# Windowed attention into an ELU feed-forward layer: v and k loaded as float32 by ScalarE's queue and cast by GpSimd, q and k transposed by DMA, a new static order

## The chip, the cores and the metric

The kernel runs on 1 core of a Trainium2 chip. The metric is the device time of one execution in microseconds (us). A core has five engines with instruction queues of their own: PE (TensorE, matmuls and transposes), DVE (VectorE), ACT (ScalarE), POOL (GpSimd) and SP (SyncE, which only issues DMAs here). ACT and POOL issue DMAs too, and an engine that issues one does so in its place among its other instructions.

## The reference

```python
# q, k, v: [8 batches, 8 heads, 576 tokens, 64] float32
scores = q @ k.transpose(0, 1, 3, 2) / 8
scores = where(abs(pos[:, None] - pos[None, :]) <= 32, scores, -1e9)
attn = softmax(scores)                       # per row
x = (attn @ v).transpose(0, 2, 1, 3).reshape(4608, 512)
h = x @ w_in                                 # [512, 2048]
g = where(h > 0, h, exp(minimum(h, 0)) - 1)  # ELU
out = g @ w_out                              # [2048, 512], float32
```

All arrays come and go as float32; the kernel computes in bfloat16 with float32 accumulation.

## The kernel before

**Units of work.** A batch is nine blocks of 64 queries (`QB`). A block of queries sees the 128 keys from 32 before it to 32 behind it. Two blocks are a *pair* of 128 tokens: 36 pairs, four and a half to a batch. Pairs are gathered into ten *tiles* of the feed-forward layer: tiles 0 and 1 have two pairs each (256 tokens), tiles 2 to 9 four (512 tokens).

**Attention.** For each batch, q and k come as float32 by four DMAs (`load_qk`, L155; half the heads each; 96 partitions, 6 tokens to a partition), issued by SP for batch 0 and by ACT later. `cast` (L168, L170) makes bfloat16 of them, on POOL from batch 1 on. `T` (L180) transposes them on PE, six matmuls against the identity for one pair of heads, eight such groups to a batch; `E` (L193 on ACT, L195 on DVE) copies each group out of PSUM into `kT` and `qT`. v comes by POOL's queue, cast to bfloat16 on the way (`load_v`, L203), the even blocks only; the odd blocks are the same rows moved by half the partitions, copied inside SBUF by DVE in batches 0 and 1 (`copy_v`) and by two DMAs of SP later (`shift_v`, L210, L212). For each pair: `QK` (L239) computes the transposed scores into `psS`, `SM` (L247, ACT) their exponential, `MK` (L260, DVE) multiplies by the mask into `pm`, `AV` (L272, PE, two groups of heads) multiplies by v, where a column of ones gives the row sums, `RN` (L285, L287, DVE) divides by them. `X` turns the pair's result round into `xt`, tokens in the free dimension: by PE for the first four pairs (L302, L308), by a DMA transpose of SP for the others (L298).

**Feed-forward.** For each tile and each of 16 slices of 128 hidden features: `H` (L319) is four matmuls into one of three `psH` buffers, `EX` (L327, ACT) the exponential, `FF` (L339, DVE; L337, ACT, for the odd slices of tiles 0 and 1) cuts it at zero, `GG` (L348 or L345, DVE) takes the larger of it and h and so frees the `psH` buffer. `Y` (L362) accumulates 16 matmuls for one pair of the tile before, in four parts of four; `YC` (L368, ACT) copies the result and `OUT` (L373, SP) stores it. Both weight matrices are loaded in four pieces each by POOL's queue, with a cast (`WI` L394, `WO` L399).

**What sets the order.** Nothing is scheduled while the kernel runs. The class `Plan` takes every operation with an engine, a duration, a rank and what it depends on, plays them through once while the program is built, and emits them in the order of this play; each engine then runs its list in that order and waits with semaphores. Where an engine stands at an instruction whose operand is not there, all that is behind it on that engine waits too. `H`'s in PE's list are mixed with `Y`'s of the tile before and with the attention of pairs about a tile ahead.

Of the kernel before, what the change touches and what calls it, by code (L numbers as in the profile page):

```python
# [20 lines left out]
class Plan:  # L21
# [4 lines left out]
    LAT = 0.25  # L26

    def __init__(self):
        self.ops = {}

    def op(self, name, eng, dur, rank, deps, fn, dma=0.0, lag=0.0,
           at=0.0):


        self.ops[name] = (eng, dur, rank, tuple(deps), fn, dma, lag, at)

    def run(self):
        ops = self.ops
        done, users, left = {}, {}, {}
        for n, o in ops.items():  # L40
            left[n] = len(o[3])
            for d in o[3]:
                assert d in ops, (n, d)
                users.setdefault(d, []).append(n)
        free = {}
        server = 2.0
        ready = {}
        for n, o in ops.items():
            free.setdefault(o[0], 0.0)
            if left[n] == 0:  # L50
                ready.setdefault(o[0], {})[n] = 0.0
        order = []
        while len(order) < len(ops):
            best = None
            for e, rs in ready.items():
                if not rs:
                    continue
                t = max(free[e], min(rs.values()))
                n = min((ops[n][2], n) for n, r in rs.items() if r <= t)[1]
                if best is None or t < best[0]:  # L60
                    best = (t, e, n)
            t, e, n = best
            del ready[e][n]
            _, dur, _, _, fn, dma, lag, at = ops[n]
            free[e] = t + dur
            if dma:
                server = max(server, t + dur) + dma
                end = server + 2.0 + lag
            else:
                end = t + dur + lag  # L70
            end = max(end, at)
            done[n] = end
            order.append((t, n))
            for u in users.get(n, ()):
                left[u] -= 1
                if left[u] == 0:
                    ue = ops[u][0]
                    r = max(done[d] + (0.0 if ops[d][0] == ue
                                       and not (ops[d][5] or ops[d][6] or ops[d][7]) else self.LAT)
                            for d in ops[u][3])  # L80
                    ready.setdefault(ue, {})[u] = r
        self.done = done
        self.order = order
        for _, n in order:
            ops[n][4]()
# [3 lines left out]
def kernel(  # L89
# [20 lines left out]
    PR = 96  # L110
    TPP = S // PR
    KW = S + 2 * WIN
# [4 lines left out]
    VW = D + 1  # L117

    const = ctx.enter_context(tc.tile_pool(name="const", bufs=1))
    stg = ctx.enter_context(tc.tile_pool(name="stg", bufs=4))  # L120
    bfp = ctx.enter_context(tc.tile_pool(name="bfp", bufs=4))
# [12 lines left out]

    ident = const.tile([128, 128], BF16)
    masks = const.tile([128, 4, QB], BF16)
# [3 lines left out]
    NVB = 3  # L140
    NPB = 2
    kT = [const.tile([128, HP, KW], BF16, name=f"kT{i}") for i in range(NKB)]
    qT = [const.tile([128, HP, S], BF16, name=f"qT{i}") for i in range(NKB)]
    vw = [const.tile([128, NQB, H, VW], BF16, name=f"vw{i}") for i in range(NVB)]
    pm = [const.tile([128, H, 3 * QB], BF16, name=f"pm{i}") for i in range(NPB)]

    live = {}
    EVAC = {(nm, hp): "DVE" if (nm, hp) == ("k", 3) else "ACT"
            for nm in "qk" for hp in range(HP)}


    def load_qk(b, nm, half, eng):
        src = {"q": q, "k": k}[nm]
        t = stg.tile([PR, HP, TPP * D], FP32, name="stg", tag="stg")
        eng.dma_start(  # L155
            out=t, in_=src[b, half * HP:(half + 1) * HP].rearrange(
                "h (p t) d -> p h (t d)", t=TPP))
        live[nm, b, half] = t

    def cast(b, nm, half, eng):  # L160
        if (nm, b) not in live:
            live[nm, b] = bfp.tile([PR, TPP, H, D], BF16, name="bf", tag="bf")
        t = live[nm, b]
        src = live.pop((nm, b, half)).rearrange("p h (t d) -> p h t d", t=TPP)
        dst = t[:, :, half * HP:(half + 1) * HP, :].rearrange(
            "p t h d -> p h t d")
        if eng is nc.scalar:
            nc.scalar.copy(dst, src)  # L168
        else:
            eng.tensor_copy(dst, src)  # L170

    def T(b, nm, hp):
        src = live[nm, b]
        n = 2 * hp + (nm == "k")
        if b == 0 and n % 4:
            pt = psH_p.tile([128, TPP, PR], BF16, name="psH", tag="psH")
        else:
            pt = psT_p.tile([128, TPP, PR], BF16, name="psT", tag="psT")
        for j in range(TPP):
            nc.tensor.transpose(pt[:, j, :], src[:, j, 2 * hp:2 * hp + 2, :],  # L180
                                ident[0:PR, 0:PR])
        live["T", b, nm, hp] = pt

    def E(b, nm, hp):
        pt = live.pop(("T", b, nm, hp))
        if nm == "k":
            dst = kT[b % NKB][:, hp, WIN:WIN + S]
        else:
            dst = qT[b % NKB][:, hp, :]
        dst = dst.rearrange("c (p t) -> c p t", t=TPP)  # L190
        src = pt.rearrange("c t p -> c p t")
        if EVAC[nm, hp] == "ACT":
            nc.scalar.copy(dst, src)  # L193
        else:
            nc.vector.tensor_copy(dst, src)  # L195


    def load_v(b, qb):
        vt = vw[b % NVB]
        vb = v[b].rearrange("h s d -> s h d")  # L200
        lo, hi = max(0, qb * QB - WIN), min(S, qb * QB - WIN + 128)
        r = lo - (qb * QB - WIN)
        nc.gpsimd.dma_start(out=vt[r:r + hi - lo, qb, :, 0:D], in_=vb[lo:hi])  # L203

    def swapped(b, qb):
        return b < 2 and qb % 2 == 1

    def shift_v(b, w0, w1):
        vt = vw[b % NVB]
        nc.sync.dma_start(out=vt[0:QB, w0:w1 - 1:2],  # L210
                          in_=vt[QB:128, w0 - 1:w1 - 1:2])
        nc.sync.dma_start(out=vt[QB:128, w0:w1 - 1:2],  # L212
                          in_=vt[0:QB, w0 + 1:w1:2])

    def copy_v(b, w0, w1, part, eng):


        vt = vw[b % NVB]
        if part == 0:
            eng.tensor_copy(vt[0:QB, w0:w1 - 1:2], vt[0:QB, w0 + 1:w1:2])  # L220
        else:
            eng.tensor_copy(vt[QB:128, w0:w1 - 1:2],
                            vt[QB:128, w0 - 1:w1 - 1:2])


    def QK(i):
        psS = psS_p.tile([128, 2, 2, HP, QB], FP32, name="psS", tag="psS")
        for s in range(2):
            b, qb = divmod(2 * i + s, NQB)
            for h in range(H):  # L230
                hp, base = h // 2, 64 * (h % 2)
                rhs = qT[b % NKB][base:base + 64, hp, qb * QB:qb * QB + QB]
                lo = qb * QB
                if swapped(b, qb):
                    parts = ((0, QB, lo + QB), (QB, 128, lo))
                else:
                    parts = ((0, 128, lo),)
                for p0, p1, c in parts:
                    nc.tensor.matmul(  # L239
                        psS[p0:p1, h % 2, s, hp, :],  # L240
                        lhsT=kT[b % NKB][base:base + 64, hp, c:c + p1 - p0],
                        rhs=rhs, start=True, stop=True)
        live["S", i] = psS

    def SM(i):
        pu = pup.tile([128, 2, 2, HP, QB], BF16, name="pu", tag="pu")
        nc.scalar.activation(pu, live.pop(("S", i)), AX.Exp, scale=SCALE)  # L247
        live["U", i] = pu

    def MK(i):  # L250
        pu = live.pop(("U", i))
        p = pm[i % NPB]
        for s in range(2):
            b, qb = divmod(2 * i + s, NQB)
            m = masks[:, 1 if qb == 0 else 2 if qb == NQB - 1 else
                      3 if swapped(b, qb) else 0, :]
# [73 lines left out]
    def fact(t, fo):  # L330
        return t < 2 and fo % 2 == 1
# [43 lines left out]

# [9 lines left out]
    NC0 = 4  # L385

    P = Plan()
# [13 lines left out]


    PER = 8.0
    LEAD = 20.0

    def prank(i):
        return PER * tiles[where[i][0]][0] + PER * (i - tiles[where[i][0]][0]) - LEAD - 16

    casts0 = {("q", 0): "DVE", ("k", 0): "ACT", ("q", 1): "DVE",
              ("k", 1): "POOL"}  # L410
    engs = {"DVE": nc.vector, "ACT": nc.scalar, "POOL": nc.gpsimd}
    cdur = {"DVE": 1.2, "ACT": 1.5, "POOL": 1.5}
    LAND = {(0, "k", 0): 6.2, (0, "q", 0): 8.7, (0, "k", 1): 11.0,
            (0, "q", 1): 14.0, (1, "k", 0): 33.0, (1, "q", 0): 36.0,
            (1, "k", 1): 39.0, (1, "q", 1): 42.0}
    SVOF = {}
    L1AT = 2
    for b in range(B):
        need = prank(b * NQB // 2)
        r0 = need - 60  # L420
        t0 = where[b * NQB // 2][0]
        early = [("H", max(t0 - 2, 0), 2 if b == 2 else 8)] if b > 1 else []
        for half in range(2):
            for nm in ("q", "k"):
                deps = list(early)
                if b == 1:
                    deps.append(("SM", L1AT))
                if b:
                    deps.append(("C", b - 1, nm, half))
                P.op(("L", b, nm, half), "ACT" if b else "SP", 0.1,  # L430
                     r0 + half, deps,
                     lambda b=b, nm=nm, half=half: load_qk(
                         b, nm, half, nc.scalar if b else nc.sync),
                     dma=0.0 if b < 2 else 2.2,
# [228 lines left out]
```

The softmax here doesn't subtract the row's maximum and nothing guards it: scores larger than these inputs give would overflow.

## Time and profile before

| | |
|---|---|
| time, two runs | 366.52 and 367.85 us, median 367.19 |
| profiled execution | span 364.3 us from the first to the last instruction; the page gives no other time of it, so 2.9 us lie between its span and the median of the runs |
| PE busy | 315.6 us (87%) |
| DVE busy | 253.8 us (70%) |
| ACT busy | 185.0 us (51%) |
| POOL busy | 87.8 us (24%) |
| TensorE clock granted, mean | 0.986 |
| DMA queues, share of 16 engines' span | POOL's (q0) 32.6%, SP's (q1) 22.3%, ACT's (q10) 18.4% |
| PE matmuls of `T` (L180, into psT and psH) | 25.5 and 3.6 us busy |
| ACT's copies of `E` (L193), DVE's (L195) | 35.6 and 6.1 us busy |
| POOL casts of q and k (L170) | 42.9 us busy, 29 of them |
| POOL DMA issues for v (L203) | 35.5 us busy, 40 of them |

A PE busy share is not PE at its peak, since each matmul's recorded time holds the tail of the pipeline too. The DMA shares add the times of packets that overlap on one engine. POOL's spans are rough.

### The profile page before, as it was taken

The numbers are of one execution on the slowest core, as the hardware profiler recorded it, in microseconds if no ns is written. First come the engines' busy times: TensorE is split into PE (matmuls) and PEld (weight loads), VectorE is DVE, ScalarE is ACT, GpSimd is POOL, SyncE is SP. The second block draws the span as 40 slices with busy tenths as digits, with TensorE's granted clock in tenths as the row PEclk, the third lists the DMA queues.
The fourth block names the chain that finished last, engine by engine and source line by source line (L and its number), as shares of the span: only waits on it lengthen the run. The fifth ranks groups of instructions, "written<-read, shape, count | busy, mean of one in ns | idle before, by whom it ended". The sixth has DMA issues, their size and how long they took to land.

```text
span 364.3 us, 7149 instructions
## 1 busy us (share of the span) xinstructions
PE 315.6 (87%) x2789; PEld 170.0 (47%) x2832; DVE 253.8 (70%) x561; ACT 185.0 (51%) x310; POOL 87.8 (24%) x97
## 2 busy tenths in 40 slices
PE   1378777975976999999899989999999999999996
PEld 1266554642433544554455445444544444444442
DVE  5467857732897769786976798679778777756610
ACT  4257757632543654665465546654664535443321
POOL 8822704950045007200710240014000000000000
PEclk9999989998998999999999999999999999999999
DMA  8999799999797359985883784186112121111012
GB/s 190 182 200 227 109 223 254 113 141 196 141 250 85 32 157 198 146 133 156 202 85 60 192 166 103 43 223 133 40 44 71 45 59 43 45 40 47 31 58 86
DMA packets 80417, 45.08 MB, mean 124 GB/s; under 512 B 56320, under 2 KB 75776, under 8 KB 80384
## 3 DMA queue, kind: packets, MB, share of 16 engines
q0 software_dynamic: 41728, 8.92, 32.6%
q1 hardware_dynamic: 27456, 19.19, 22.3%
q10 hardware_dynamic: 11200, 16.52, 18.4%
q8 instruction: 22, 0.36, 0.5%
q14 instruction: 11, 0.09, 0.1%
HBM read 36.70 MB, written 9.44 MB: 127 GB/s over the span
## 4 chain that ended last, share of the span: by engine, by line
PE 55%; DVE 19%; DMA 15%; issue 3%; ACTq 3%; POOL 2%; ACT 2%; POOLq 0%; DVEq 0%
PE psH L319 23%; PE psY L362 21%; DVE f L339 6%; DVE g L348 5%; DMA xt<-xs 5%; DMA stg<-in_q_dram 4%; DMA w_out_sb<-in_moe_w_out_dram 4%; DVE pm L260 4%; PE psO L272 3%; PE psT L180 3%; DVE xs L287 3%; ACTq L155 3%; DMA vw<-in_v_dram 2%; PE psS L239 2%; PE psO L362 1%
## 5 line engine op out<-in xcount | busy, mean ns | idle before, releaser
L319 PE MATMUL psH<-xt,w_in_sb 128*128 128x512 bf16 (+1 forms) x626 | 148.4, 364 | 12.5 <-DMA xt<-xs 5.4
L327 ACT ACTIVATE e<-psH 128x512 f32<-128x512 f32 (+1 forms) x160 | 87.8, 554 | 116.7 <-PE psH L319 96.0
L362 PE MATMUL psY<-w_out_sb,g 128*128 128x512 bf16 x499 | 130.0, 380 | 7.7 <-DMA w_out_sb<-in_moe_w_out_dram 4.4
L339 DVE TENSOR_SCALAR f<-e 128x512 bf16<-128x512 f32 (+1 forms) x144 | 71.3, 495 | 48.7 <-ACT e L327 48.4
L348 DVE TENSOR_TENSOR g<-psH,f 128x512 bf16<-128x512 f32 (+1 forms) x144 | 95.3, 662 | 4.8
L319 PEld LDWEIGHTS <-w_in_sb 128*128 128x128 bf16 x640 | 60.7, 99 | 69.4 <-issue 18.0
L362 PEld LDWEIGHTS <-g 128*128 128x128 bf16 x576 | 51.8, 98 | 58.2 <-issue 6.4
L170 POOL CAST bf<-stg 96x1536 bf16<-96x1536 f32 x29 | 42.9, 1478 | 126.1 <-DMA stg<-in_k_dram 112.3
L203 POOL DMA_DIRECT2D vw<-in_v_dram x40 | 35.5, 897 | 37.1 <-PE psO L272 34.3
L247 ACT ACTIVATE pu<-psS 128x1024 bf16<-128x1024 f32 x36 | 36.7, 1020 | 7.2 <-PE psS L239 6.0
L272 PE MATMUL psO<-vw,pm 128*128 128x65 bf16 x544 | 30.5, 197 | 8.2 <-DVE pm L260 6.3
L272 PEld LDWEIGHTS <-pm 128*128 128x128 bf16 x576 | 26.8, 101 | 23.0 <-DVE pm L260 10.8
L260 DVE TENSOR_TENSOR pm<-pu,masks 128x512 bf16<-128x512 bf16 x72 | 33.1, 502 | 6.0 <-ACT pu L247 5.9
L180 PEld LDWEIGHTS <-bf 96*128 96x128 bf16 x384 | 24.2, 104 | 25.5 <-ACT bf L168 7.5
L287 DVE TENSOR_TENSOR xs<-psO,rc 128x256 bf16<-128x256 f32 x68 | 28.9, 425 | 3.3 <-DMA xt<-xs 1.0
L180 PE MATMUL psT<-ident,bf 96*128 96x96 bf16 x348 | 25.5, 211 | 4.9 <-DVE bf L170 4.9
L368 ACT COPY y<-psY 128x512 f32<-128x512 f32 x33 | 19.3, 586 | 14.8 <-PE psY L362 9.9
L193 ACT COPY qT<-psT 128x576 bf16<-128x576 bf16 x30 | 19.1, 636 | 11.9 <-PE psT L180 11.8
L285 DVE RECIPROCAL rc<-psO 128x4 f32<-128x4 f32 x68 | 12.1, 178 | 14.2 <-PE psO L272 14.0
L239 PE MATMUL psS<-qT,kT 64*128 64x64 bf16 (+1 forms) x640 | 17.0, 199 | 2.3 <-ACT pu L247 1.9
L239 PEld LDWEIGHTS <-kT 64*128 64x128 bf16 (+1 forms) x640 | 12.1, 102 | 13.3 <-issue 11.9
L193 ACT COPY kT<-psT 128x576 bf16<-128x576 bf16 x21 | 13.4, 638 | 9.7 <-PE psT L180 9.7
(46 smaller groups left out, 75.0 us busy)
## 6 DMA issues: line engine op xcount, KB each, us to landing
out_dram<-y SPq DMA_DIRECT2D x36, 256.0 KB, 2.0
stg<-in_k_dram ACTq DMA_DIRECT2D x14, 576.0 KB, 9.0
stg<-in_q_dram ACTq DMA_DIRECT2D x14, 576.0 KB, 11.2
vw<-vw SPq DMA_DIRECT2D x12, 260.0 KB, 4.5
vw<-in_v_dram POOLq DMA_DIRECT2D x24, 128.0 KB, 8.3
w_in_sb<-in_moe_w_in_dram POOLq DMA_DIRECT2D x4, 512.0 KB, 10.0
w_out_sb<-in_moe_w_out_dram POOLq DMA_DIRECT2D x4, 512.0 KB, 12.5
vw<-in_v_dram POOLq DMA_DIRECT2D x16, 96.0 KB, 8.8
```

What stands on the lines that cost most here:

```text
L170: eng.tensor_copy(dst, src)
L180: nc.tensor.transpose(pt[:, j, :], src[:, j, 2 * hp:2 * hp + 2, :], ident[0:PR, 0:PR])
L239: nc.tensor.matmul(psS[p0:p1, h % 2, s, hp, :], lhsT=kT[b % NKB][base:base + 64, hp, c:c + p1 - p0], rhs=rhs, start=True, stop=True)
L247: nc.scalar.activation(pu, live.pop(("S", i)), AX.Exp, scale=SCALE)
L260: nc.vector.tensor_mul(dst, pu[:, :, s], mb)
L272: nc.tensor.matmul(o[:, j, :], lhsT=p[:, h, s * QB:s * QB + 128], rhs=vw[b % NVB][:, qb, h, :], start=(s == 0), stop=(s == 1))
L287: nc.vector.tensor_mul(live["X", i][:, g * HP:(g + 1) * HP, :], o[:, :, 0:D], rb)
L319: nc.tensor.matmul(ps, lhsT=w_in_sb[:, do, fo * 128:(fo + 1) * 128], rhs=xts[t][:, do, :], start=(do == 0), stop=(do == NDO - 1))
L327: nc.scalar.activation(e, ps, AX.Exp)
L339: nc.vector.tensor_scalar(f, e, -1.0, 0.0, ALU.add, ALU.min)
L348: nc.vector.tensor_tensor(gs[t][:, fo, :], ps, f, ALU.max)
L362: nc.tensor.matmul(ps, lhsT=gs[t][:, fo, c * 128:(c + 1) * 128], rhs=w_out_sb[:, fo, :], start=(fo == 0), stop=(fo == NFO - 1))
```

## The change

**Loads and casts.** v no longer comes by POOL's queue with a cast. ACT issues five DMAs a batch (`load_v`) of float32, one token to a partition, 256 bytes a packet, into one buffer `vs` for all batches; POOL casts them into `vw` by three copies for each (`cast_v`: an even block, and the two halves of the odd block, which replaces `copy_v` and `shift_v`); in batch 0 DVE, ACT and POOL share these casts. `vw` has two buffers instead of three. k of batches 2 to 7 comes the same way: five DMAs of ACT a batch (`load_k`), five casts of POOL (`cast_k`). q, and k of batches 0 and 1, come as before but with 8 tokens to a partition: 72 partitions and runs of 2048 bytes instead of 96 and 1536 (`load_st`), three buffers instead of four, cast in two parts.

**Transposes.** q and k of batches 2 to 7 are transposed by SP: five DMA transposes for k (`xk`, 128x512 each, the last 64x512) and four for q (`xq`, 80x1024 each) a batch, in place of `T` and `E`. Batches 0 and 1 keep `T` (eight matmuls of 72 columns instead of six of 96) and `E`. `qT` is kept in the order that these transposes leave, and `QK` and `SM` read it by strides. Odd blocks of batches 0 and 1 are no longer computed in swapped halves, so `QK` has 16 matmuls throughout.

**ELU.** `FF` moves from DVE to ACT for every fourth slice of tiles 2 to 9.

**Order.** `Plan` is new: it plays DMA rings that share the bandwidth, buffers that are taken and given back, and other durations. Loads of a batch are released by a slice of an earlier tile (`gate`). The zeroing of buffers and the masks are now operations of the plan. The weights' DMAs stay with POOL, `w_out`'s without a dependency, `w_in`'s behind the third load of v.

The core of the diff:

```diff
-    def load_qk(b, nm, half, eng):
...
-    def shift_v(b, w0, w1):
...
+    def load_st(b, nm, half, eng):
+        src = {"q": q, "k": k}[nm]
+        t = stg.tile([NP, HH, TP * D], FP32, name="stg", tag="stg")
+        eng.dma_start(
+            out=t, in_=src[b, half * HH:(half + 1) * HH].rearrange(
+                "h (p t) d -> p h (t d)", t=TP))
...
+    def xq(b, half, part):
+        src = bf[bfm(b, "q", half) % NBF]
+        n = TP * HH * D // 2
+        dst = qT[b % NKB][:, half, part * TP // 2:(part + 1) * TP // 2].rearrange(
+            "c t j p -> c (t j) p")[:, :, PL:PL + NPZ]
+        nc.sync.dma_start_transpose(dst, src[:, part * n:(part + 1) * n])
...
+    def load_k(b, j, eng):
+        n = min(128, S - 128 * j)
+        t = ksp.tile([128, H * D], FP32, name="ks", tag="ks")
+        eng.dma_start(
+            out=t[0:n].rearrange("p (h d) -> p h d", h=H),
+            in_=k[b].rearrange("h s d -> s h d")[128 * j:128 * j + n])
...
+    def cast_k(b, j, eng):
...
+        kb = kbp.tile([128, H * D], BF16, name="kb", tag="kb")
+        eng.tensor_copy(kb[0:n], t[0:n])
...
+    def xk(b, j):
...
+        nc.sync.dma_start_transpose(
+            kT[b % NKB][:, :, WIN + 128 * j:WIN + 128 * j + n], kb[0:n])
...
+    def load_v(b, e, eng):
+        vb = v[b].rearrange("h s d -> s h d")
+        lo, hi = max(0, 2 * e * QB - WIN), min(S, 2 * e * QB - WIN + 128)
+        r = lo - (2 * e * QB - WIN)
+        eng.dma_start(
+            out=vs[r:r + hi - lo, e, :].rearrange("p (h d) -> p h d", h=H),
+            in_=vb[lo:hi])
+
+    def cast_v(b, e, part, eng):
+        vt = vw[b % NVB]
+        sv = vs.rearrange("p e (h d) -> p e h d", h=H)
+        if part == 0:
+            dst, src = vt[:, 2 * e, :, 0:D], sv[:, e]
+        elif part == 1:
+            dst, src = vt[0:QB, 2 * e + 1, :, 0:D], sv[QB:128, e]
+        else:
+            dst, src = vt[QB:128, 2 * e + 1, :, 0:D], sv[0:QB, e + 1]
...
     def fact(t, fo):
-        return t < 2 and fo % 2 == 1
+        return fo % 2 == 1 if t < 2 else fo % 4 == 3
...
+        gate = []
+        if b == 1:
+            gate = [("H", 0, 8)]
+        elif b > 1:
+            gate = [("H", where[first(b - 2)][0] + (b == 2), 8)]
+        for e in range(NVE):
...
+            P.op(("LV", b, e), "ACT", 0.35, -1990 + e if b == 0 else need - 110 + e, deps,
+                 lambda b=b, e=e: load_v(b, e, nc.scalar), dma=("A", 64, 22))
...
+            P.op(("L", b, nm, half), eng, 0.4,
+                 -1990 + n if b == 0 else need - 95 + n, deps,
...
+                P.op(("LK", b, j), "ACT", 0.35, need - 98 + j, deps,
...
+                P.op(("CK", b, j), "POOL", 0.6, need - 60 + j, deps,
...
+                P.op(("XK", b, j), "SP", 1.2, need - 46 + j,
...
+        P.op(("WI", c), "POOL", 0.8, -990 + c, [("LV", 0, 2)], lambda c=c: WI(c), dma=("P", 32, 98))
+        P.op(("WO", c), "POOL", 0.8, -890 + c, [], lambda c=c: WO(c), dma=("P", 32, 98))
```

What this gives in the lists: for each of batches 3 to 7 ACT's list has an unbroken row of eleven DMA issues (five of v, four of k, two of q) and a twelfth further on, where it had four; in batch 1 a row of eight, in batch 2 a row of eleven that stands among the copies out of PSUM of batch 1. POOL's list has 13 casts of v, five of k and four of q a batch. SP's has nine transposes a batch among the `X`'s and the stores.

## Prediction

> **What bounds the kernel now.** I read the page first, for the span, the engines' shares and the 40 slices.
>
> ```profile
> span 364.3 us, 7149 instructions
> ...
> PE 315.6 (87%) x2789; PEld 170.0 (47%) x2832; DVE 253.8 (70%) x561; ACT 185.0 (51%) x310; POOL 87.8 (24%) x97
> ...
> PEclk9999989998998999999999999999999999999999
> DMA  8999799999797359985883784186112121111012
> ```
>
> PE is the engine with most work, but the DMA row says that this changes over the span: nines until about 90 us, little from 250 us on. So I asked for busy time by stage, cut where tile 2's `H` begins (85.98 us) and where the page's PE row becomes steady.
>
> ```profile
> 85.80:120.00 34.20, 28.17 (x219) 13.58 (x223) 27.13 (x56) 15.57 (x25) 9.44 (x8) 0.91 1.02 161
> 120.00:284.00 164.00, 157.20 (x1411) 81.99 (x1433) 130.38 (x274) 92.40 (x146) 33.24 (x27) 1.00 0.60 120
> 284.00:364.30 80.30, 75.44 (x453) 35.29 (x460) 44.61 (x93) 31.60 (x51) 0.00 (x0) 1.00 0.16 51
> ```
>
> The columns are the length, then busy time of PE, PE's weight loads, DVE, ACT and POOL, the granted clock, DMA share, GB/s. From 120 us PE is busy for 157.2 of 164.0 us and 75.4 of 80.3: there, taking work from PE gains it in full, and whatever makes PE wait costs in full. Before 86 us PE waits for loads. Then the timeline, first of PE at the turn of the stages:
>
> ```profile
> 85.98 1.86 PE L319 MATMUL psH<-xt,w_in_sb 128*128 128x512 bf16 x4 [5.45 <-DMA xt<-xs]
> 88.07 2.05 PE L319 MATMUL psH<-xt,w_in_sb 128*128 128x512 bf16 x7 [0.22 <-issue]
> ```
>
> After 5.45 us of idling four matmuls take 1.86 us, where four take 0.86 elsewhere, and the next seven 2.05 instead of 1.5: a long wait costs some 1.6 us more behind it, at the lower clock. Last, all engines around ACT's row of loads:
>
> ```profile
> 128.75 0.42 PE L180 MATMUL psT<-ident,bf 96*128 96x96 bf16 x6
> ...
> 129.01 1.03 PE L362 MATMUL psY<-w_out_sb,g 128*128 128x512 bf16 x4
> ...
> 130.14 0.32 ACTq L155 DMA_DIRECT2D stg<-in_k_dram  x1
> ...
> 130.57 0.42 ACTq L155 DMA_DIRECT2D stg<-in_q_dram  x1
> ...
> 131.08 0.43 ACTq L155 DMA_DIRECT2D stg<-in_k_dram  x1
> ...
> 131.61 1.48 ACTq L155 DMA_DIRECT2D stg<-in_q_dram  x1
> ...
> 133.20 0.60 ACT L327 ACTIVATE e<-psH 128x512 f32<-128x512 f32 x1 [2.54 <-PE psH L319]
> ...
> 134.76 0.41 PE L239 MATMUL psS<-qT,kT 64*128 64x64 bf16 x16 [0.82 <-ACT pu L247]
> ```
>
> Two things are to be seen. A group of `T` keeps PE for 0.26 us (128.75 to 129.01), its 0.42 holds the pipeline's tail. And four DMA issues keep ACT from any `EX` for 2.95 us, the fourth alone for 1.48; PE then waits, for 0.82 us here. In 130 to 133.1 us the queue moved 202 packets of the 1600 issued (400 to a load): the fourth issue ended with some 90 packets per DMA engine still to come.
>
> **The change, part by part.** The sum is made against the profiled execution, span 364.3; the median of the runs is 367.19, so 2.9 are added at the end.
>
> *Transposes off PE.* 48 groups go, 0.26 us each. The eight of batch 2 lay before 86 us, where PE waited anyway; 40 count: 40 x 0.26 = **-10.4**. Batches 0 and 1 keep as many columns (8x72 for 6x96), nothing. The swapped halves of `QK` fall before 62 us, nothing. The copies taken from ACT (42 of 0.64) and DVE (6 of 0.76) gain only where these engines hold PE. `FF`'s move puts 32 pieces (0.50 each on DVE) on ACT, at most 0.83 (twice the 0.417 of half the width): 27 us back for 27 gone. DVE's lists stay under 75%. I cost these at nothing; the cover is the three `psH` buffers.
>
> *ACT's row of eleven issues.* In batches 3 to 7 it stands between two `EX`. Nothing in the trace shows a fifth issue. From below: eleven at the pitch of the first ones (0.48) take 5 us. From above: if no more than about 90 packets per engine may wait, as at the end of the fourth issue, the rest must have moved first. A load of v or k is 1024 packets of 256 bytes, 64 per engine and one for the semaphore; nine of these and two of q make 635, less 90 are 545, or 8.4 loads. The nearest row for the pace is v itself, loaded in before:
>
> ```profile
> q0 software_dynamic: 2025, 0.26, 200.6%
> ```
>
> That is the window 68 to 70 us, POOL's queue almost alone: 2025 packets in 2 us, a load of 1024 in 1.0. So 8.4 us and 1.1 until the first packet: 9.5. The order of the changed kernel adds that SP's and ACT's DMAs take eight completion counters in turn, and that q's loads wait in mid-row for the third (batch 3: the fifth) load of v, about 5 to 7 us after the first. I take **8**, nearer the end with the fourth issue's evidence. Behind the row stand three `EX`, and for them PE.
>
> PE's cover, from the changed lists: between the first issue and the first matmul that needs ACT's work from behind the row, PE has 3.5, 4.3, 6.5, 5.2 and 6.0 us in batches 3 to 7 (`H` and `Y` 0.86, `QK` 0.42, `AV` 0.23), in all 25.5. It resumes 2.0 after the row: `EX` 0.60, `FF` 0.43, `GG` 0.69, hand-overs. Idle: 5 x (8 + 2.0) - 25.5 = 24.5; before's rows cost about 1 each, 5. Net **+19.5**, between +4.5 (row of 5) and +27 (9.5). Three of the five waits are then long enough for the lower clock, 3 x 1.6: **+5** (0 to 8).
>
> The Trainium skill speaks against this part: "Perfetto Trace Analysis", section "DMA Instruction — HWDGE (DVE, Sync)", says that the issuing sequencer is held until the generator, which ACT and SP share, has made all descriptors of the DMA, and that a full descriptor buffer makes the engines start before that. The rule gives no size of the buffer; read strictly it makes the row 9.5 us and the net +27, a reading of the first issues alone gives +4.5.
>
> *Start of tile 2* (85.98 in before). Later: the `w_in` pieces, issued behind `w_out` and behind a cast that needs two v loads; batch 1's loads, issued at 23.9 us in before and now held for the ninth slice of tile 0, about 37 us (first `H` at 28.6 in before, some 3 later now). The page's list of DMA issues lands such a load 9 to 11 us after issue, and the fourth waits for POOL's 13 casts of v and two of k. So batch 1's copies end near 64 instead of 55, and the row of batch 2 stands among them. Earlier: no POOL loads of v between 64 and 86 us, which filled the DMA engines while an `X` took 9 us; all weights by about 45 instead of 58. Five pairs at 2 us, then `X` behind four transposes of q on SP (1.2 x 640/512 = 1.5 each). I take **87**, from 80 to 95: +1.0.
>
> *POOL's casts.* 1.48 for 1536 columns gives 0.49 for a v or k cast and 0.99 for half a q: some 95, 30 and 32 of them, 94 us instead of 43. They collide with DVE:
>
> ```profile
> 138.98 1.48 POOL L170 CAST bf<-stg 96x1536 bf16<-96x1536 f32 x1
> ...
> 139.33 1.42 DVE L260 TENSOR_TENSOR pm<-pu,masks 128x512 bf16<-128x512 bf16 x1
> ```
>
> `MK` ends with the cast; its median is 0.418. Means over minima on DVE (84 ns x 72 `MK`, 75 x 128 `FF`) make 16 us lost to 43 of casts, so 34 to 94. Most hides under PE; I take **+3** (0 to 10).
>
> *DMA and SP queues.* q and k: nine transposes a batch at 1.2 to 1.5 us put 11.6 us of issuing on SP ahead of `X` and `OUT`, which run a tile ahead of PE (28 us). Packets of a batch: 9 x 1.0 + 2 x 2.5 on ACT's queue, of 37 us. I cost this at nothing; without that cover the first `X` of a tile comes up to 11.6 us late, which at tile 2 is the third rival. The stage 86 to 120 lost 6 us of PE and 3 of clock to late loads; part of that goes: **-6** (0 to -9).
>
> Sum: 364.3 - 10.4 + 19.5 + 5 + 1 + 3 - 6 = 376.4; with 2.9, **379**.
>
> **The rivals.** *The row is short.* All eleven issues pass at 0.48, 5 us. For it: the first three do, and at the start SP's four took 0.40 to 0.48 each. Against: ACT's fourth never did. Then +4.5 without lower clock and without DVE's loss, tile 2 at 83: 364.3 - 10.4 + 4.5 - 3 - 8 = 347.4, **350**. It decides from rows under 6 us.
>
> *The row is twice as long.* Two queues share the engines packet for packet: from 30 to 35 us q0 and q10 moved 738 each. With SP's transposes beside it v runs at half its pace: 8.4 x 2.0 + 1.1 = 18. Idle 5 x 20 - 25.5 - 5 = 69.5, clock 8, tile 2 at 95: **446**. Against: transposes do not run throughout.
>
> *The chain of batches 1 and 2 is the trouble*: `QK` of pair 9 stands ahead of tile 2's first `H` in PE's list, and needs batch 2's transposes, these POOL's casts, these `AV` of pair 4. If each waits its worst, tile 2 starts at 100: **392**.
>
> **How the numbers follow.** Forecast 0.54 (own range 362 to 398), short row 0.24, double row 0.10, chain 0.12. The time is the forecast's, 379. The range is 347 to 414: it leaves out the double row and the lower part of the short row. Two per cent, about what a measurement tells from no change, are 359.8 and 374.5. Faster: 0.21 of the short row and 0.01 of the forecast, 0.22. Within: 0.03 and 0.13, 0.16. Slower: 0.40, 0.10 and 0.12, 0.62.
>
> **What would show it.** ACT's issues of a row, first to last: 8 us right, under 6 the first rival, over 14 the second. PE idle before the first `H` behind each row, 3 to 7 us, its releaser DVE's g or ACT's e. Tile 2's first `H` at 80 to 95. `T` only in batches 0 and 1. MK's mean above 0.55. The forecast is wrong if PE is as busy from 120 us as before.

## The result, and the profile after

The changed kernel takes 429.58 us (428.58 to 430.59) against 367.19: a ratio of 1.170, 95% interval 1.161 to 1.178. The forecast was 379 with a range of 347 to 414. The direction was right; the loss, 62.4 us, was about five times the forecast one of some 12. The profiled execution has a span of 426.9 us, 62.6 more than before. First the page: span, shares, granted clock and DMA share in 40 slices.

```profile
span 426.9 us, 6767 instructions
...
PE 313.8 (74%) x2471; PEld 161.5 (38%) x2512; DVE 233.0 (55%) x516; ACT 180.9 (42%) x304; POOL 123.7 (29%) x181
...
PEclk9999989759779599699986996999699999999999
DMA  7998096794527988955496579667975211110112
```

PE does 318 matmuls fewer and is busy for nearly as long (313.8 against 315.6), in a longer span: 113 us idle instead of 49. The clock's row shows one reason why the fewer matmuls save so little: from the eighth slice to the twenty-ninth it dips again and again, down to 5, where before had nines almost throughout, and each matmul of `H` and `Y` is longer there (the step on the lower clock below has the numbers).

Then busy time by stage, cut where tile 2 begins (118.85 us; before 85.98) and where the last row of loads begins (columns as in the prediction's table).

```profile
118.85:165.00 46.15, 35.91 (x240) 16.73 (x246) 29.79 (x65) 20.82 (x34) 15.51 (x22) 0.85 0.78 121
165.00:293.00 128.00, 101.89 (x814) 49.54 (x828) 78.40 (x169) 54.68 (x86) 48.43 (x66) 0.88 0.77 152
293.00:426.90 133.90, 120.58 (x786) 56.53 (x799) 72.84 (x154) 60.41 (x99) 15.66 (x22) 0.97 0.34 84
```

In the steady part PE is busy for 80% (101.89 of 128.00) at a mean clock of 0.88; before it was 96% at 1.00. So the loss has two halves: tile 2 begins 32.9 us later, and from there to the end it takes 29.7 us longer. The releasers of PE's waits, longest first (engine, what waits, what it waited for: sum, times, longest):

```profile
PE psH L419 <- DVE g L448: 28.5, 8, 7.5
PE psH L259 <- ACT bf L245: 18.9, 2, 17.7
PE psO L372 <- DVE xs L387: 14.6, 10, 8.0
PE psS L338 <- ACT pu L346: 10.9, 5, 7.0
PE psT L259 <- ACT kT L272: 9.5, 1, 9.5
```

DVE's `GG` and ACT's `SM` are named, but they are the messengers. The timeline of ACT and PE at batch 4 shows what made them late:

```profile
165.80 3.97 ACTq L310 DMA_DIRECT2D vs<-in_v_dram  x5
169.89 4.38 ACTq L287 DMA_DIRECT2D ks<-in_k_dram  x4
174.31 1.65 ACTq L234 DMA_DIRECT2D stg<-in_q_dram  x2
176.06 0.60 ACT L427 ACTIVATE e<-psH 128x512 f32<-128x512 f32 x1 [9.64 <-POOL vw L326]
...
170.24 0.41 PE L338 MATMUL psS<-qT,kT 64*128 64x64 bf16 x16
177.62 0.61 PE L338 MATMUL psS<-qT,kT 64*128 64x64 bf16 x16 [6.98 <-ACT pu L346]
178.34 1.87 PE L419 MATMUL psH<-xt,w_in_sb 128*128 128x512 bf16 x4
```

Eleven issues hold ACT from 165.80 to 175.96 with pauses of 0.12 us at most between them; the name of POOL at the end of ACT's idle time is only that of the latest event. PE runs out of work 4.8 us after the row began, and the four matmuls of `H` behind the wait take 1.87 us, where four took 1.03 before it (164.10 us, same view). The other half of the loss begins at the start, again PE and ACT:

```profile
9.45 0.68 PE L259 MATMUL psH<-ident,bf 72*128 72x72 bf16 x8
27.84 1.14 PE L259 MATMUL psH<-ident,bf 72*128 72x72 bf16 x16 [17.71 <-ACT bf L245]
...
8.01 18.63 ACTq L310 DMA_DIRECT2D vs<-in_v_dram  x3
26.74 1.04 ACT L245 CAST bf<-stg 72x1024 bf16<-72x1024 f32 x1 [17.81 <-issue]
```

Three issues of v for batch 0 keep ACT for 18.63 us. Behind them stands the cast of q that PE's transposes need.

### The profile page after: what moved, and what is told of

Read it like the earlier page. It is cut to its first block, busy times and chain, and to the rows that moved or that the text cites. A ratio compares the mean times of both kernels' runs of the same rounds, so it can differ in the third digit from the quotient of the medians.

```text
span 426.9 us, 6767 instructions
## 1 busy us (share of the span) xinstructions
PE 313.8 (74%) x2471; PEld 161.5 (38%) x2512; DVE 233.0 (55%) x516; ACT 180.9 (42%) x304; POOL 123.7 (29%) x181
## 4 chain that ended last, share of the span: by engine, by line
PE 52%; DMA 12%; ACTq 10%; DVE 9%; ACT 8%; issue 4%; SPq 3%; POOL 3%; POOLq 0%; DVEq 0%
PE psH L419 24%; PE psY L462 18%; ACTq L310 7%; DMA ks<-in_k_dram 4%; PE psO L372 3%; ACT e L427 3%; DVE pm L360 2%; POOL vw L326 2%; DMA vs<-in_v_dram 2%; SPq L281 2%; PE psS L338 2%; ACTq L287 2%; DVE xs L387 2%; DVE g L448 2%; DVE f L439 1%
## 5 line engine op out<-in xcount | busy, mean ns | idle before, releaser
L419 PE MATMUL psH<-xt,w_in_sb 128*128 128x512 bf16 (+1 forms) x617 | 155.8, 378 | 32.6 <-DVE g L448 28.5
L462 PE MATMUL psY<-w_out_sb,g 128*128 128x512 bf16 x511 | 134.4, 385 | 3.6 <-ACT y L468 1.8
L439 DVE TENSOR_SCALAR f<-e 128x512 bf16<-128x512 f32 (+1 forms) x112 | 51.2, 461 | 90.1 <-ACT e L427 90.0
L326 POOL CAST vw<-vs 64x512 bf16<-64x512 f32 (+1 forms) x95 | 60.6, 639 | 127.6 <-DMA vs<-in_v_dram 118.1
L448 DVE TENSOR_TENSOR g<-psH,f 128x512 bf16<-128x512 f32 (+1 forms) x112 | 72.3, 650 | 2.9
L346 ACT ACTIVATE pu<-psS 128x1024 bf16<-128x1024 f32 x36 | 36.9, 1024 | 22.2 <-PE psS L338 22.2
L372 PE MATMUL psO<-vw,pm 128*128 128x65 bf16 x544 | 29.8, 200 | 15.0 <-DVE xs L387 14.6
L445 DVE SCALAR_TENSOR_TENSOR g<-f,psH 128x512 bf16<-128x512 bf16 (+1 forms) x48 | 28.6, 595 | 20.7 <-ACT f L437 20.6
L372 PEld LDWEIGHTS <-pm 128*128 128x128 bf16 x576 | 27.3, 103 | 30.9 <-DVE xs L387 18.7
L296 POOL CAST kb<-ks 128x512 bf16<-128x512 f32 (+1 forms) x30 | 20.3, 682 | 63.1 <-DMA kT<-kb 35.6
L247 POOL CAST bf<-stg 72x1024 bf16<-72x1024 f32 x32 | 34.9, 1124 | 4.6 <-ACT qT L272 3.1
L338 PE MATMUL psS<-qT,kT 64*128 64x64 bf16 x576 | 17.4, 205 | 17.9 <-ACT pu L346 10.9
L437 ACT ACTIVATE f<-e 128x512 bf16<-128x512 f32 (+1 forms) x48 | 26.8, 558 | 1.4
L338 PEld LDWEIGHTS <-kT 64*128 64x128 bf16 x576 | 12.6, 103 | 31.8 <-issue 25.7
L385 DVE RECIPROCAL rc<-psO 128x4 f32<-128x4 f32 x68 | 12.2, 179 | 20.6 <-PE psO L372 19.8
L259 PEld LDWEIGHTS <-bf 72*128 72x128 bf16 x128 | 7.7, 123 | 41.1 <-ACT bf L245 28.2
```

Source lines behind the costliest of these rows:

```text
L338: nc.tensor.matmul(psS[:, h % 2, s, hp, :].rearrange("k (t p) -> k t p", t=TP), lhsT=lhs, rhs=rhs, start=True, stop=True)
L346: nc.scalar.activation(pu.rearrange("k a s h (p t) -> k (a s h) p t", t=TP), src, AX.Exp, scale=SCALE)
L372: nc.tensor.matmul(o[:, j, :], lhsT=p[:, h, s * QB:s * QB + 128], rhs=vw[b % NVB][:, qb, h, :], start=(s == 0), stop=(s == 1))
L419: nc.tensor.matmul(ps, lhsT=w_in_sb[:, do, fo * 128:(fo + 1) * 128], rhs=xts[t][:, do, :], start=(do == 0), stop=(do == NDO - 1))
L439: nc.vector.tensor_scalar(f, e, -1.0, 0.0, ALU.add, ALU.min)
L448: nc.vector.tensor_tensor(gs[t][:, fo, :], ps, f, ALU.max)
```

## The experiments

Each kernel was timed beside the kernel before (366.3 to 368.9 us); but for the last there is one time each, and the seventeen times of the kernel before beside the last one lie between 362.7 and 368.6; so a difference of a few us between two kernels is not read. The table gives the first exponential of tiles 0, 1 and 2 and the span, in us, so that a gain can be put in its place; the last column is the stretch from tile 2 to the end.

| kernel | tile 0 | tile 1 | tile 2 | span | from tile 2 |
|---|---|---|---|---|---|
| before | 29.7 | 42.6 | 87.9 | 364.3 | 276.4 |
| changed | 46.6 | 66.2 | 120.7 | 426.9 | 306.2 |
| e_v0_sp | 35.8 | 57.5 | 109.5 | 417.9 | 308.4 |
| e_wo_late | 31.2 | 52.8 | 102.7 | 408.1 | 305.4 |
| e_spread | 47.4 | 63.5 | 109.3 | 392.6 | 283.3 |
| e_t_only | 47.6 | 68.4 | 110.5 | 405.9 | 295.4 |
| e_wl_spread | 31.1 | 50.4 | 100.1 | 385.7 | 285.6 |
| e_row_sp | 30.9 | 44.3 | 101.7 | 381.4 | 279.7 |
| e_best3 | 31.4 | 55.0 | 82.9 | 371.8 | 288.9 |
| e_best3_t | 32.6 | 55.8 | 80.2 | 363.2 | 283.0 |

**What holds an issue (m_row).**

> Only loads, none of the reference's work. Five rows of twelve DMA issues, each row begun when the one before has landed: A 1024 packets of 256 bytes a load, ACT alone; B half of that; C 1024 packets of 512 bytes; D 144 packets of 2048 bytes on 72 partitions; E six loads as in A on ACT and six on SP together. Theory 1 (room): an issue ends when no more than about 2650 packets of its queue wait, so in A the first two or three issues pass in 0.3 to 0.6 us, the rest each last what 1024 packets take to move (about 1.1 us), and the row 10 to 12 us; B: five pass, the rest 0.5 to 0.6 each, row 5 to 6; C: the rest as long as 1024 packets of 512 bytes take, longer than in A; D: none is held, row 4 to 6. E: if the room is each queue's own, two or three of each pass and the rest last twice the pace of A; if it is shared, the second of each is held. Theory 2 (each descriptor costs issue time, about 1.1 ns): from the first issue on A 1.1 us each, B 0.55, C exactly as A, D 0.15 to 0.4, and E as A on each engine.

In the built order the rows A, B and C followed one another without a pause, which leaves their steady parts readable. The issues of A and of C, in us, in order:

```
A (256-byte packets)  0.42 0.61 0.84 0.88 1.15 1.15 1.16 1.16 1.10 1.33 1.15 1.15
C (512-byte packets)  0.58 1.59 1.65 1.69 1.69 1.69 2.02 1.83 1.62 1.96 1.69 1.69
```

C has the same number of packets as A and holds ACT 1.5 times as long, and A's first two issues are shorter than the rest; neither fits theory 2, one price for each descriptor. The DMA view of ACT's queue (packets begun, MB, share) over row A, 0.73 to 13.19 us:

```profile
q10 hardware_dynamic: 9964, 2.51, 117.2%
```

Twelve loads are 12,480 packets (16 of each load are for its completion), so 2516 still waited when the last issue ended; at the end of C it was 2411 (31,296 issued, 28,885 begun). With packets of 256 and 512 bytes an issue in such a row ended when about 2500 packets of its queue still waited; I call this the room. The same view of the changed kernel, from the first issue of batch 4 to the end of its ninth (165.80 to 174.27):

```profile
q10 hardware_dynamic: 6230, 1.57, 109.8%
```

8848 issued less 6230 is 2618: the same room.

Two rows do not fit this number. In B the first issue took 1.11 behind what A had left, and the others 0.60 to 0.68 while only 1715 to 2050 packets waited (at its end 2047: 18,816 issued, 16,769 begun). These were not held by the room: a load of k of the same 64 rows takes 0.62 to 0.69 in the changed kernel with its queue empty. D's loads of 144 packets of 2048 bytes passed in 0.31 to 0.35, as theory 1 has it, but for the first: it took 1.94, and when it ended 1398 packets waited (31,456 issued, 30,058 begun), far fewer than 2500. The fourth load of a row in the kernel before, of 1536-byte packets, was held until as few were left (1600 less 202), and when batch 4's row ended, with q's two loads of 2048-byte packets, 1774 waited (9456 less 7682). So with larger packets a load is held for longer than the count of 2500 says; what sets the room there, no run settles.

E told less than meant: its issues were kept apart by waits for completion counters. One place in it speaks on the room: at 64.67 us ACT's issue took 0.48 and SP's 0.37 while 1502 and 2080 packets waited behind them, 3582 in all, so the room seems to be each queue's own.

**The start: whose packets (e_v0_sp, e_wo_late).**

```diff
-            P.op(("LV", b, e), "ACT", 0.35, -1990 + e if b == 0 else ...
+            # e_v0_sp: batch 0 on SP, behind its q and k
+            P.op(("LV", b, e), "ACT" if b else "SP", 0.35, -1980 + e if b == 0 else ...
...
-        P.op(("WO", c), "POOL", 0.8, -890 + c, [], ...
+        # e_wo_late
+        P.op(("WO", c), "POOL", 0.8, -890 + c, [("WI", NWC - 1)], ...
```

> The five v loads of batch 0 are issued by SP behind its four loads of q and k, not by ACT; all else as in the changed kernel. Theory (ACT's row holds the copies behind it): no wait of 17 us of PE before 28 us; the first H at 30 to 34 instead of 45.6 us, and the time 411 to 420 against 429.6. Rival (w_out's loads take the engines at the start, whoever issues v): first H after 40 us, time 424 or more.

> w_out's four loads are issued by POOL behind w_in's instead of ahead of all; ACT's row of five v loads in batch 0 stays. Theory (row, drained at the pace that the engines leave to it): without w_out's packets the row ends near 17 instead of 26.6 us, first H at 35 to 40, time 418 to 424. Rival (w_out alone made the start late): first H at 28 to 31, time 409 to 414. If w_out takes no part: nothing changes.

Measured: 419.64 and 409.84. Taking the row off ACT brought tile 0 forward by 10.8 us, at the weak edge of what the row theory said (the first `H` came at 34.8; SP was held for 16.94 us by the same five loads); taking w_out's packets away brought 15.4 us with the row still on ACT, which only the rival foresaw. ACT in e_wo_late:

```profile
6.44 1.62 ACTq L310 DMA_DIRECT2D vs<-in_v_dram  x3
...
8.09 5.50 ACTq L310 DMA_DIRECT2D vs<-in_v_dram  x2
13.68 1.04 ACT L245 CAST bf<-stg 72x1024 bf16<-72x1024 f32 x1 [4.96 <-DVE bf L247]
```

The row ends at 13.59 instead of 26.64 us. Both are causes, in series: ACT stands because its queue has no room, and the room came so slowly because POOL's packets of w_out (1024 bytes each) took the engines. From 8.0 to 15.9 us in the changed kernel ACT's queue began 526 packets, POOL's 775 and SP's 513; in batch 4's row ACT's began 6230 in 8.5 us.

**The rows (e_spread, e_row_sp, e_t_only).** Three ways to the same question. e_spread makes single issues of the rows, e_row_sp (with w_out late) keeps them as rows but on SP, e_t_only keeps them on ACT and makes them shorter.

```diff
-            gate = [("H", where[first(b - 2)][0] + (b == 2), 8)]
+        def slot(n, b=b):                       # e_spread: load n of batch b
+            t0 = 0 if b == 1 else where[first(b - 2)][0] + (b == 2)
+            t1, fo = divmod(4 + n, NFO)
+            return [("H", t0 + t1, fo)]
...
-                P.op(("LK", b, j), "ACT", ...   # e_row_sp: LV, LK and L alike, b > 0
+                P.op(("LK", b, j), "SP", ...
...
-    NBPE = 2                                    # e_t_only
+    NBPE = 8
```

> From batch 1 on each load of ACT is released by a slice of its own (from the 4th slice of the same tile on), so that the rows of eight and eleven issues fall apart into single issues between the exponentials; the number of issues, casts and transposes is unchanged, and so is the start. Theory (rows): PE's waits of 7 to 8 us in batches 3 to 7 go, and the lower clock behind them: 38 + 9 us less, and some 10 of the waits in batches 1 and 2: 372 to 392. Rival (the chain of loads, casts and SP's transposes sets the pace): the waits move to transposes of q and k, less than 12 us gained, 415 or more.

> w_out's loads behind w_in's, and the rows of loads from batch 1 on kept as rows but issued by SP; ACT issues v of batch 0 alone. Theory (a row does harm through what stands behind it on its engine): SP is now held for 10 to 13 us a batch, ACT not; behind SP's row stand the X of a later tile and the stores, which have a tile of time (28 us): 370 to 388 against 409.8 with the rows on ACT. Rival (what is late are the loads, casts and transposes themselves): 400 or more, with X or the transposes of q as the releaser of PE's waits.

> The changed kernel with one part undone: T and E of all batches stay on PE, ACT and DVE, k comes like q, SP transposes neither; gates, order of the weights and ACT's rows of v and q, k stay. A row has five v loads and up to four of 304 packets each, about 5900 packets instead of 9456. Theory (rows priced by packets beyond some 2600 that may wait, at 1.1 us for 1024): rows of 5 to 7 us instead of 10 to 12.5, PE's waits behind them 2 to 4 instead of 7 to 8, some 27 us less with the clock, 11.5 us of T back: 405 to 416. Rival (the transposes by DMA are a large part of the loss in themselves): under 400. Start as in the changed kernel, first H near 46.

e_spread: 394.36, 35 us less and 2 above the theory's bound; far from the rival's. Its loads each take what an issue takes when the queue has room, and the exponentials run between them:

```profile
145.24 0.34 ACTq L310 DMA_DIRECT2D vs<-in_v_dram  x1
146.33 0.60 ACT L427 ACTIVATE e<-psH 128x512 f32<-128x512 f32 x1 [0.47 <-PE psH L419]
146.33 0.41 ACTq L310 DMA_DIRECT2D vs<-in_v_dram  x1
148.06 0.60 ACT L427 ACTIVATE e<-psH 128x512 f32<-128x512 f32 x1 [1.13 <-PE psH L419]
```

The stretch from tile 2 falls by 22.9 us, and tile 2 comes 11.4 earlier. A new wait in ACT's list kept it from gaining more:

```profile
211.96 0.64 ACTq L287 DMA_DIRECT2D ks<-in_k_dram  x1
212.70 0.60 ACT L427 ACTIVATE e<-psH 128x512 f32<-128x512 f32 x1 [10.17 <-DMA kT<-kb]
```

An exponential does not read `kT`. The load of k ahead of it waited in place, and the releaser is a transpose issued by SP: ACT waits on the counter (semaphore 118 in the trace) that the load will use and that a transpose into `kT`, issued at 199.57 us, used last; that transpose landed at 211.89. Two such waits, the other at a load of q, cost ACT 16.1 us, and PE stood 5.3 and 8.0 us behind them.

e_row_sp: 383.15, 26.7 less than e_wo_late with the same rows (409.84). SP is now held as ACT was, 143.20 to 154.08 us for one of its rows:

```profile
143.20 3.88 SPq L310 DMA_DIRECT2D vs<-in_v_dram  x5
147.12 5.82 SPq L287 DMA_DIRECT2D ks<-in_k_dram  x4
152.98 1.10 SPq L234 DMA_DIRECT2D stg<-in_q_dram  x2
```

From tile 2 on PE hardly notices (279.7 us where e_wo_late took 305.4), since `X` and the stores behind SP's row have a tile of time. This is the cleanest sign that a row costs through what stands behind it on its engine. Ahead of tile 2 it is no gain: what it wins between tiles 0 and 1 (13.3 us against 21.6 with the rows on ACT) it loses between 1 and 2 (57.4 against 49.9).

e_t_only: 407.71, as expected. From the first to the eighth issue the rows of batches 3 to 7 take 6.0, 5.5, 6.9, 6.0 and 6.1 us and PE waits 4.6, 1.9, 3.0, 2.0 and 1.9 behind them, 2.7 in the mean. With before's rows of 2.95 us (0.3 us of wait in the mean) and the changed kernel's of 11.6 (7.3), the wait grows by 0.8 us for each us of row between the two longer ones: PE's cover is used up, and nearly all that is added is paid.

**Both edits together (e_wl_spread).** w_out late and single issues.

> Both edits in one kernel: w_out's loads behind w_in's, and ACT's loads from batch 1 on spread one to a slice. Alone they gave 409.8 and 394.4 against 429.6. Theory (two separate losses, the start and the rows): the gains add, 394.4 - 19.8 = 374.6, between 370 and 380; first H of tile 0 near 30 us. Rival (the chain of casts and transposes behind the loads takes over once both are gone): 385 or more.

387.38, as the rival had it: the gains do not add (19.7 and 35.2 alone, 42.2 together). Tile 2 comes 20.6 us earlier where the two edits alone make 29.4, so most of what is missing lies ahead of tile 2; its cause was not looked for. Behind tile 2 one load of k waits in place for 8.7 us, again for a counter, this time of a transpose of `X`, and PE stands for 6.7:

```profile
127.26 0.63 ACTq L287 DMA_DIRECT2D ks<-in_k_dram  x1
127.99 0.60 ACT L427 ACTIVATE e<-psH 128x512 f32<-128x512 f32 x1 [8.70 <-DMA xt<-xs]
```

**Towards a better version (e_wl_spread3, e_best3, e_best4, e_best6).**

```diff
-    ksp = ctx.enter_context(tc.tile_pool(name="ksp", bufs=4))
+    ksp = ctx.enter_context(tc.tile_pool(name="ksp", bufs=5))       # e_wl_spread3
-            t1, fo = divmod(4 + n, NFO)
+            t1, fo = divmod(2 + n, NFO)                             # e_wl_spread3; n: v, k, q
-            deps = slot(...)
+            deps = [("SM", n)] if b == 1 else slot(...)             # e_wl_spread3, L of q and k
+            le = "ACT" if b else "SP"                               # e_best3, LV as in e_v0_sp
+            t0 = 0 if b <= 2 else where[first(b - 2)][0]            # e_best4, slices from 10 on
+            le = "ACT" if b == 1 else "SP"                          # e_best6 on e_best3: LV, LK and L
```

> As both edits together, and: five buffers for k instead of four, so that the last k load needs no cast before it; loads of a batch in the order v, k, q, from the 2nd slice on; q and k of batch 1 released by the first four exponentials of scores instead of slices of tile 0. Theory (in the spread kernel ACT waited 16 us at two loads for completion counters last used by SP's transposes, and tile 2 waited for batch 1's loads): these waits go and tile 2's first H comes before 92 us instead of about 101: 352 to 368. Rival: the waits move to other loads, no better than 372.

> The same as the one before, and v of batch 0 issued by SP behind q and k. Theory: with w_out's packets gone ACT's row at the start held it for some 4 us only, so 0 to 5 us less than the kernel without this edit: 350 to 366. Rival (v behind q comes too late for the first A times V): 0 to 5 more.

> The last kernel, with the loads of batch 2 released by slices of tile 0 (from the 10th on) instead of tile 1. In the last kernel pairs of tile 3 ran behind all H of tile 2, with PE waiting between them (83 to 130 us, 47 us for tile 2 where before took 30). Theory (batch 2's loads, casts and transposes are late there): tile 3 starts 8 to 15 us earlier, time 358 to 367. Rival (tile 2 moves later by as much, since batch 1's casts and batch 2's share POOL): 371 to 378.

> The last kernel, with the loads of batches 2 to 7 issued by SP, still one to a slice, instead of ACT. Theory (what is left of ACT's loss are waits in place for completion counters and casts): ACT has no such waits, 366 to 372. Rival (SP's transposes and X, in order behind these waits, come late instead): 376 or more.

Measured: 383.75, 373.52, 374.49 and 368.02. The first two missed their forecasts (352 to 368 and 350 to 366), the first as its rival had it. In e_wl_spread3 tile 2 came forward as foreseen (90.8 against 100.1 in e_wl_spread), but 5.6 of these 9.3 us were lost again behind it (291.2 from tile 2 to the end); v of batch 0 on SP was worth 10 us, not 5; batch 2's earlier loads were worth nothing (the rival); and moving the loads to SP gave 5.5 more, within its forecast, but no more than the times of before differ among themselves. "The last kernel" in the expectations of e_best4, e_best6 and e_best3_t is e_best3. What holds tiles 2 and 3 back in e_best3 (from 82.9 to 130.1 us where before took 30) was not settled.

**The transposes (e_best3_t, e_best7).** `NBPE = 8` in e_best3, and the same with the loads of batches 2 to 7 on SP.

> The last kernel with T and E kept on PE, ACT and DVE for all batches: k comes like q in runs of eight tokens, no transposes of q and k by SP. Theory (the transposes off PE are worth their columns once the rows are gone): 48 groups of 0.24 us back on PE, less some 4 us of waits for transposes: 377 to 386 against 373.5. Rival (loads as single tokens, casts and transposes by DMA cost as much as they save): 373 or less.

> All edits that helped: w_out behind w_in, v of batch 0 and all loads from batch 2 on by SP, one to a slice, q and k of batch 1 early, T and E kept on PE, ACT and DVE. Against the kernel with T kept and the loads on ACT (365.3 in one look) ACT loses nine issues of 0.35 to 0.45 us a batch and its waits in place: 358 to 365, ratio to before 0.975 to 0.995. Rival (X late behind SP's loads): 366 or more, ratio 1.0 or above.

e_best3_t: 365.31, faster by 8.2 than the same kernel with the transposes by DMA. The rival was right: the part of the change that I had booked as its gain is a loss here, taken with what belongs to it (k as single tokens, their casts, nine transposes of SP), from which one pair of times does not separate it. PE in e_best3 and then in e_best3_t:

```profile
PE 311.2 (84%) x2472; PEld 160.4 (43%) x2512; DVE 245.8 (66%) x516; ACT 181.0 (49%) x304; POOL 122.9 (33%) x181
```

```profile
PE 317.2 (87%) x2850; PEld 171.3 (47%) x2896; DVE 244.7 (67%) x522; ACT 204.3 (56%) x346; POOL 131.3 (36%) x175
```

Without `T` PE has 6.0 us less work and 14.6 us more idling (60.6 against 46.0). Most of that can be named: waits for SP's transposes into `xt` and `kT` fall from 10.0 to 2.5 us, and those of `AV` for `RN` from 6.7 to 3.0. The Trainium skill, "VectorE: DVE Perf Modes", section "Rules for kernel authors", says of a 128x128 transpose to do it on TensorE where the result may go to PSUM and by DMA otherwise. These two runs agree, 365.3 against 373.5 us, though their transposes are of 72 or 80 rows or of 128x512 and the loads of k differ too.

e_best7: median 363.36 us of twelve times, against 366.59 of seventeen of before. The ratio on record, which leaves out the one slowest time here and the two slowest of before, is 0.994, interval 0.990 to 0.998. It is the best version here, by half a per cent, well under the two per cent that the prediction takes as no change. It keeps of the change the loads of v and the casts on POOL, runs of eight tokens, `FF`'s share on ACT and the new planner.

## Why the prediction was wrong, step by step

The sum was 376.4; the profiled execution took 426.9, 50.5 more. 31.9 of that lie before tile 2 and 18.6 behind it.

**Start of tile 2: +1.0 forecast, +32.9 measured. This step failed.** I wrote that the first `H` would come "some 3 later" and counted "all weights by about 45 instead of 58" on the gain side. It came 16.9 later, before and then changed:

```profile
28.62 1.01 PE L319 MATMUL psH<-xt,w_in_sb 128*128 128x256 bf16 x4 [0.38 <-ACT xt L308]
```

```profile
45.56 1.01 PE L419 MATMUL psH<-xt,w_in_sb 128*128 128x256 bf16 x4 [0.23 <-ACT xt L408]
```

The rule that I applied to batches 3 to 7, that issues hold the engine until packets move, applied in batch 0 as well, where three issues took 18.6 us with casts and copies behind them; and w_out's loads without a dependency were the reason why packets moved so slowly (e_wo_late gave back 15.4 us of it). The two working together were in the lists and I priced neither. The rest, another 16 us, I had priced only through the arrival of data, and most of it are the rows of batches 1 and 2: tile 0 took 6.7 longer with a wait of 4.7 behind the row of eight, tile 1 took 9.2 longer with one of 9.5 behind the row of eleven, and e_spread, which takes these rows apart, gave back 11.4. My worst case of the chain rival, tile 2 at 100, was short by 19.

**ACT's row: 8 us forecast, 11.6 measured; a term mis-sized.** The rows take 11.6, 10.2, 12.5, 12.2 and 11.5. The mechanism was the one forecast, and PE waited 8.0, 7.0, 7.5, 6.9 and 7.1 there, 36.4 in all; my formula with the measured rows gives 5 x (11.6 + 2.0) - 25.5 = 42.5, so it is a little too hard. Before's five rows, for which I took off 5, cost PE 0.6, 0.8 and nothing that shows in the other three, 1.4. The net is 35.0 against 19.5.

The row was mis-sized at several places. A load of 1024 packets takes 1.1 us in the clean row of batch 4, not the 1.0 read from POOL's queue; the first packet comes some 1.6 us after the first issue, not 1.1. The four other rows, in which more of SP's packets stand (688 to 1776 against 295), are 1.3 to 2.3 us longer; in batch 6 some 2 of that are two waits for completion counters between the issues. The room of 90 packets per engine came from loads of 1536-byte packets and was taken over to packets of 256 bytes, where it was 2618 / 16, or 164. And I counted 635 packets per engine where the row has 591 (9456 in all: two of the five loads of v have 96 rows, and q's loads 304 packets). The last two errors made the row longer and hid part of the first ones. That I took 8 and not the bound of 9.5 gave weight to the three fast issues, which only show that the room was still empty. The page that I cited for this part ("Perfetto Trace Analysis", the same section) was nearer than my choice: the ninth issue of batch 4 was held for 1.11 us and ended with 2618 packets not begun, as behind a full buffer of that depth. The page gives no size for the room, and it names DVE and Sync as the ones that share the generator, not ACT and SP.

**Relief of the stage before 120 us: -6 forecast, 2.8 found.** Apart from the waits behind the rows, PE stands idle for 13.3 us behind the start of tile 2, against 16.1 in before. PE's busy time there is 2.4 less (258.4 against 260.8): that is `T`'s 10.4 off, if it is taken as forecast, and the 8 of the next step on. The forecast's -10.4, +5 and +3 make the same 2.4 by luck, since the clock took what the casts did not. So the 18.6 behind tile 2 are the 15.5 of the row and the 3.2 missing here, to 0.1.

**Lower clock: +5 forecast.** `H` and `Y` together, with as many records, are busy for 290.2 us (155.8 and 134.4 on the page) against 278.4: about 12, of which 8 lie behind the start of tile 2 (263.2 against 254.9). The step was right in kind and low, since every wait was longer. The 1.6 us that I took for one long wait were a little high, too, as they set times with the pipeline's tail (1.86) against times without it (0.86).

**Transposes off PE: -10.4 forecast.** `T` is left in batches 0 and 1 only, 128 matmuls, as forecast. But I costed SP's nine transposes a batch at nothing, with `X` and `OUT` "a tile ahead" as the cover. Once rows were gone, that cover was too thin: 14.6 us of idling for 6.0 of work, in kernels that differ in the loads and casts of k as well. The columns were right and the term of nothing was wrong, though the rows hid it in the changed kernel.

**POOL's casts: +3 forecast.** `MK` takes 0.554 us in the mean, from 0.502 (forecast: above 0.55), 3.7 us over 72 of them, on an engine that is busy for 55%. The sign that I named came; what it cost in time no run shows. The casts themselves take 115.8 us (60.6, 34.9 and 20.3 on the page), not 94.

**The rivals.** The row was as long as the second rival had it only where w_out's packets shared the engines, at the start (18.6 us for three issues), and POOL's queue began 775 packets there to ACT's 526, not one for one. The short row fell: nothing of eleven issues passed in under 10 us.

## What to carry to other kernels

Count packets, not issues: here a DMA issue took some 0.3 to 0.9 us while its queue had room and about as long as the transfer of a whole load once it had none (1.1 to 1.2 us for 1024 packets of 256 bytes, up to 7.9 at the start), and then everything behind it on that engine waits. Such rows belong on an engine with slack behind them, or are to be spread one issue to a slot; and the rule must be applied to every row in the list, first of all at the start, where all queues share the engines. Work taken off the bounding engine is a gain only if the path that replaces it has time to spare: price that path before booking the gain.

## What the runs showed of the hardware that was not expected

- With packets of 256 and 512 bytes ACT's queue took in about 2500 of them before an issue was held (2516 and 2411 in m_row, 2618 in the changed kernel): twice the bytes gave nearly the same count, and an issue of 1.69 us instead of 1.15. With larger packets the count was lower: 1398 in before (1536 bytes) and at the first load of m_row's row D (2048 bytes).
- A load of 64 rows (512 packets) took 0.60 to 0.69 us to issue without being held, longer than the 0.42 of a load of 128 rows into an empty queue.
- At the start another queue's packets of 1024 bytes slowed ACT's queue from some 730 packets per us (6230 in 8.5 us) to 67 (526 in 7.9 us), with SP's loads beside it.
- A load on ACT can wait 8.7 to 10.2 us for a transpose issued by SP with which it shares nothing but a completion counter.
